# First and second down product of a block summed in PSUM, and the down products reordered

## The chip, the cores and the metric

The kernel runs on one core of one Trainium2 chip. The metric is the time of one execution in microseconds on the device, as the median of several runs. One execution was also taken by the hardware profiler; all views below are of that execution. The engines are named as in the profile: PE is TensorE's matmul, PEld its weight load, DVE is VectorE, ACT is ScalarE, POOL is GpSimd and SP is SyncE, which issues most loads.

## The reference

Input is x of 2048 rows and 512 columns. It is normalised by rows (layer norm without weights), and then two things are computed of it and joined. All is in 32-bit floats.

```python
xn = layernorm(x)
a  = einsum("sd,ed->se", xn, dft_hid_re)
b  = einsum("sd,ed->se", xn, dft_hid_im)
s  = dft_seq_re @ a - dft_seq_im @ b          # 2048 x 2048 matrices
g  = (sigmoid(xn @ w_gate) * (xn @ w_up)) @ w_down   # 512 -> 1792 -> 512
out = x + s * silu(g)
```

## The kernel before

**Exactness.** Every 32-bit operand of a matmul is split into a high and a low part: `split` (lines 73 and 74) rounds the value on ScalarE (`hi`) and takes the rest on VectorE (`lo`). A product is then three matmuls, hi by hi, hi by lo and lo by hi (`mm3`, lines 77 to 79). Each has 128 x 128 weights and 512 columns.

**Fewer products.** All large products are done as 2 x 2 blocks with seven block products instead of eight (the scheme of Strassen and Winograd). In the code, the seven are named 1, 6, 7, 4 (a chain that adds up in one place and is read after some of its steps), 2 (which goes on from product 1) and 5, 3 (a second chain). The sums and differences of the operands are made on VectorE (`combine`, line 129).

**Memory.** SBUF is a pool of 54 pages of 4 KB a partition (`page`); a page is used again when its last reader is done. PSUM has eight banks (`bank`): ga, ua, gb, ub, gc and uc for the chains a, b and c of the gate and up products, and two named pd for down products.

**Stages.** First 35 us normalise and turn half of the rows and do the first group of features. Then come 13 blocks (`BLOCKS`), each for one half h of the rows (1024) and one group g of 256 of the 1792 features. After them the DFT along the sequence (`seq_units`, four chunks), then that along the hidden dimension (`hidden_units`), which also multiplies with silu(g) and adds x.

**A block** (`block`) is seven units, one for each of the gate and up products in the order 1, 5, 2, 6, 7, 4, 3. A unit is twelve matmuls, six into a bank of g and six into one of u. After product 1, `seed` (line 475) copies ga and ua into gb and ub, so that product 2 can go on there. After products 6 and 7, `snap` (line 469) copies ga and ua into a page, and the next product goes on in ga and ua; `gate` (line 484) and `times` (line 487) form sigmoid(g) * u.

**Down products.** The gated block results of a block are multiplied with w_down while the next block runs: each unit of a block ends in one down product of the block before. For nearly all blocks this job is a `Seven`: seven products, each of six matmuls into the two pd banks. `SEVEN` gives their order. `run` does one; it takes new pd banks for products 2, 1 and 5 and goes on in the old ones for the others. After each product `gather` (line 309) copies both banks into a page on ScalarE, and POOL issues a DMA of 512 KB (line 311, or 314 the first time) that adds the page to one of eight parts of g in DRAM, g_part. Products 1 and 2 go to the same part (0, 0).

**Order.** The order of the instructions on every engine is written out by hand. `units` is a list of what TensorE does; `add` appends one with the operands it needs. Two units ahead of its use an operand is split, five ahead it is loaded. `sooner(n, f)` and `after(n, f)` put a step f before or after unit n. `Seven.spread` places the steps of a job relative to the first unit n of its own block: the differences and the splits of w_down (`Down.spread`; `raw` is the split of w_down itself, `dif` of its four differences), the four sums t1 to t4 of the gated results (`self.sums`), and the splits of the operands of products 6, 7 and 4. The list `waiting` holds the down products still to do; a job's seven are put there at unit 1 of the next block, and each unit takes the first one. What is left after the last block is done in chunk 0 of the DFT, after each second step of a product (`left` in `seq_units`).

**Other stores of POOL** that the prediction names: `i_part` (line 782) keeps operands of an inner product of the DFT, `s_part` (line 685) holds sums of xn, `f_part` (line 869) takes results of the first DFT, and `put_x` (line 1017) copies x into the output. SP's loads are of line 88.

Of the kernel before, what the change touches and what calls it, by code (L numbers as in the profile page):

```python
# [11 lines left out]
AF = mybir.ActivationFunctionType  # L12
# [23 lines left out]
def fnet_glu_kernel(ctx: ExitStack, tc: tile.TileContext, x, x_t, c_re, c_im, w_h, w_gu, w_down, out):  # L36
    nc = tc.nc
# [11 lines left out]
    def bank(tag):  # L49
        return banks.tile([P, 512], F32, name=tag, bufs=2 if tag == "pd" else 1)  # L50
# [25 lines left out]
    def mm3(ps, ws, ms, first, last, go_on=False):  # L76
        nc.tensor.matmul(ps, ws[0], ms[0], start=first, stop=False, skip_group_check=go_on)  # L77
        nc.tensor.matmul(ps, ws[0], ms[1], start=False, stop=False, skip_group_check=go_on)  # L78
        nc.tensor.matmul(ps, ws[1], ms[0], start=False, stop=last, skip_group_check=go_on)  # L79
# [235 lines left out]


    GATED = {(0, 0): 1, (0, 1): 2, (1, 0): 4, (1, 1): 3}
    SEVEN = (1, 6, 7, 4, 2, 5, 3)
    waiting = []

    class Plain:
# [23 lines left out]
        def run(self, n):  # L345
            b, i = divmod(n, 2)
            outs = []
            for o in range(2):
                at = slice((2 * i + o) * P, (2 * i + o + 1) * P)
                outs.append(bank("pd"))  # L350
                for f in range(2):
                    mm3(outs[-1], [t[:, at] for t in self.weights(f)], self.hs[f, b].get(), f == 0, f == 1)
            gather((2 * self.h + b) * 2 + i, outs)
# [13 lines left out]
    class Down:  # L367
# [21 lines left out]

        def spread(self, n, late):  # L390
            sooner(n + 4 * late - 4, self.wdl.load)
            for i, f in zip((4, 5, 6, 8) if late else (0, 2, 3, 5), (lambda: self.diffs(0), lambda: self.diffs(1), self.raw.get, self.dif.get)):
                after(n + i, f)

    class Seven:
# [2 lines left out]
        items, at = SEVEN, range(7)  # L398

        def __init__(self, h, wd, made):  # L400
            self.first, self.s, self.ps, self.made = 4 * h, {}, None, made
            self.raw, self.dif, self.wd = wd.raw, wd.dif, wd
            value = lambda k: lambda: self.s[k][:, 0, :]
            b11, b12, b21, b22 = (value(k) for k in (1, 2, 4, 3))

            def total(k, a, b):
                return Value([], lambda: combine(self.s[k][:, 1, :], a(), b(), ADD))

            t1 = total(1, b11, b12)
            t2 = total(3, t1.get, b22)  # L410
            t3 = total(2, b12, b22)
            t4 = total(4, t2.get, b21)
            self.sums = t1, t2, t3, t4
            src = {1: b11, 5: t1.get, 6: t2.get, 3: b22, 7: t3.get, 2: b21, 4: t4.get}
            self.h = {k: Parts([], v, [SB], joint=True) for k, v in src.items()}

        def spread(self, n, late):

            if not self.made:
                self.wd.spread(n, late)  # L420
            self.last = n == 7 * (len(BLOCKS) - 1)
            for i, v in zip((9, 11, 14, 17) if self.last else (7, 7, 8, 9), self.sums):
                sooner(n + i, v.get)
            if not self.last:
                for i, v in (8, self.dif), (8, self.h[6]), (9, self.h[7]), (10, self.h[4]):
                    sooner(n + i, v.get)

        def needs(self, k):

            if k in (6, 7, 4) and not self.last:  # L430
                return []
            return [self.h[k], self.dif if k in (5, 6, 7, 3) else self.raw]

        def weights(self, k):
# [2 lines left out]
            j, i = {1: (0, 0), 2: (1, 0), 4: (1, 1)}[k]  # L437
            return [t[:, j, i * D // 2 : (i + 1) * D // 2] for t in self.raw.get()]

        def run(self, k):  # L440
            first = k in (2, 1, 5)
            if first:
                self.ps = [bank("pd") for _ in range(2)]
            hv, wv = self.h[k].get(), self.weights(k)
            for o, ps in enumerate(self.ps):
                mm3(ps, [t[:, o * P : (o + 1) * P] for t in wv], hv, first, True, go_on=not first)
            (b, i), sign = {
                2: ((0, 0), 1),
                1: ((0, 0), 1),
                6: ((1, 0), -1),  # L450
                7: ((1, 1), -1),
                4: ((0, 1), 1),
                5: ((1, 1), 1),
                3: ((1, 0), 1),
            }[k]
            gather(self.first + 2 * b + i, self.ps, sign)

    def block(h, w, made, before, job, late):

        s, ps = job.s, {}  # L460
        n = len(units)
        if not made:
            for i, v in zip((-3, 0, 1, 3), w["s"]):
                sooner(n + i, v.get)

        def snap(k):
            s[k] = page([2, SB], F32)
            for m, c in enumerate("gu"):
                nc.scalar.activation(s[k][:, m, :], ps[c + "a"], AF.Copy)  # L469

        def seed():

            for c in "gu":
                ps[c + "b"] = bank(c + "b")
                nc.scalar.activation(ps[c + "b"], ps[c + "a"], AF.Copy)

        def plus(k):
            for m, c in enumerate("gu"):
                nc.vector.tensor_add(s[k][:, m, :], s[k][:, m, :], ps[c + "c"])

        def gate(k, tag=None):
            if tag:
                s[k] = page([2, SB], F32)
            nc.scalar.activation(s[k][:, 0, :], ps["g" + tag] if tag else s[k][:, 0, :], AF.Sigmoid)

        def times(k, tag=None):
            nc.vector.tensor_mul(s[k][:, 0, :], s[k][:, 0, :], ps["u" + tag] if tag else s[k][:, 1, :])

        tail = {1: seed, 6: lambda: snap(2), 7: lambda: (snap(3), plus(3)), 3: lambda: plus(2)}
        CH = {1: "a", 5: "c", 2: "b", 6: "a", 7: "a", 4: "a", 3: "c"}  # L490

        def unit(k, d):
            first = k in (1, 5)
            for m, c in enumerate("gu"):
                tag = c + CH[k]
                if first:
                    ps[tag] = bank(tag)
                product(k, ps[tag], w, h, m, first)
            if k in tail:
                tail[k]()  # L500
            if d:
                d[0].run(d[1])
            if k in (2, 4):
                gate({2: 1, 4: 4}[k], CH[k])
            if k in (7, 3):
                gate({7: 3, 3: 2}[k])
            if k == 4:
                times(4, "a")

        for i, k in enumerate((1, 5, 2, 6, 7, 4, 3)):  # L510
            if i == 1:
                waiting.extend((before, d) for d in before.items)
            d = waiting.pop(0) if waiting and i in waiting[0][0].at else None
            add([xop[h, k], w[k]] + (d[0].needs(d[1]) if d else []), lambda k=k, d=d: unit(k, d))
        sooner(n + 3, lambda: times(1, "b"))
        sooner(n + 5, lambda: times(3))
        sooner(n + 7, lambda: times(2))
        job.spread(n, late)
        return job
# [443 lines left out]

    def seq_units(job, c_sums):
        ops = a_operands()
        left = waiting + [(job, k) for k in SEVEN]
        n = len(units)
        after(n + 40, lambda: nc.scalar.activation(warm, mhalf, AF.Silu))
        for q in range(2):
            sooner(n - 9 + 4 * q, ops[1, q].load)  # L970
            sooner(n - 5 + 4 * q, ops[1, q].get)
        inner_a([n + i for i in (-43,-41,-38,-36,-34,-31,-27,-24,-20,-6,-3)])
        chunks = [Chunk(i, c_sums) for i in range(NT)]
        starts = []
        pair = None
        for tc_, plan in enumerate(PLAN):
            starts.append(len(units))
            c = chunks[tc_]
            done = dict.fromkeys(CHAIN, 0)
            for t in plan.replace(" ", ""):  # L980
                if t in "abcdefg":
                    if pair is None or pair.ended():
                        pair = Inner(*chunks[tc_ // 2 * 2 :][:2])
                    pair.step("abcdefg".index(t) + 1)
                    continue
                k = int(t)
                c.step(ops, k, done[k])
                done[k] += 1
                if left and done[k] % 2 == 0:
                    last_down(*left.pop(0))  # L990
        assert not left
        blocks = [Load(w_h[i, j], [4, D // 2]) for i in range(2) for j in range(2)]
        sums_ahead(diffs, blocks, w_part, range(starts[2] + 5, starts[2] + 9), 4)
# [148 lines left out]
    with tc.manual_schedule():  # L1142
        job, begin = start(0, 0)
# [102 lines left out]
```

## Time and profile before

| what | value |
|---|---|
| median of 3 runs | 804.81 us (804.71 to 805.5) |
| profiled execution | 804.79 us, span 803.0 us |
| PE busy | 794.5 us, 3594 matmuls |
| PEld busy | 658.1 us |
| DVE busy | 704.8 us |
| ACT busy | 535.9 us |
| POOL busy | 129.6 us |
| stores to g_part | 95, 512 KB each |
| granted TensorE clock | 1.00 in all windows |

The span goes from the first to the last instruction of the program; the time of the execution holds what lies around it too. Busy time is the time in which at least one instruction of an engine runs. In the list of groups, the columns are line, engine, operation, output and input, shape and count; then busy time and mean duration of one; then the idle time of the engine just before these instructions, with what ended it. The chain of waits follows the last instruction back to what released it, step by step.

### The profile page before, as it was taken

The numbers are of one execution on the slowest core, as the hardware profiler recorded it, in microseconds if no ns is written. First come the engines' busy times: TensorE is split into PE (matmuls) and PEld (weight loads), VectorE is DVE, ScalarE is ACT, GpSimd is POOL, SyncE is SP. The second block draws the span as 40 slices with busy tenths as digits, with TensorE's granted clock in tenths as the row PEclk, the third lists the DMA queues.
The fourth block names the chain that finished last, engine by engine and source line by source line (L and its number), as shares of the span: only waits on it lengthen the run. The fifth ranks groups of instructions, "written<-read, shape, count | busy, mean of one in ns | idle before, by whom it ended". The sixth has DMA issues, their size and how long they took to land.

```text
span 803.0 us, 10266 instructions
## 1 busy us (share of the span) xinstructions
PE 794.5 (99%) x3594; PEld 658.1 (82%) x3594; DVE 704.8 (88%) x917; ACT 535.9 (67%) x831; POOL 129.6 (16%) x179
## 2 busy tenths in 40 slices
PE   9999999999999999999999999999999999999997
PEld 8988888888888888788888887888887888888886
DVE  6878889889988998888989698999698899888986
ACT  4676888889777888777987855553545645548371
POOL 2002443222221223222211100001110000000201
PEclk9999999999999999999999999999999999999999
DMA  8153999997988999998999898429977585874826
GB/s 276 42 205 94 227 222 225 226 188 133 183 183 290 194 264 258 289 244 167 232 301 292 221 326 304 136 90 335 396 268 256 206 300 189 303 267 163 202 60 105
DMA packets 51139, 177.89 MB, mean 222 GB/s; under 512 B 5648, under 2 KB 5904, under 8 KB 51088
## 3 DMA queue, kind: packets, MB, share of 16 engines
q0 software_dynamic: 21696, 75.52, 43.6%
q1 hardware_dynamic: 29312, 101.66, 35.7%
q8 instruction: 28, 0.46, 0.2%
q14 instruction: 23, 0.19, 0.1%
q10 hardware_dynamic: 80, 0.07, 0.0%
HBM read 104.86 MB, written 76.03 MB: 225 GB/s over the span
## 4 chain that ended last, share of the span: by engine, by line
PE 94%; DMA 2%; DVE 2%; issue 1%; ACT 0%; DVEq 0%; ACTq 0%
PE pd L79 6%; PE pd L78 6%; PE pd L77 6%; PE ga L77 6%; PE ga L78 6%; PE ga L79 6%; PE ua L78 5%; PE ua L79 5%; PE ua L77 5%; PE gc L78 3%; PE gc L79 3%; PE uc L78 3%; PE uc L79 3%; PE uc L77 3%; PE gc L77 3%; PE gb L78 3%
## 5 line engine op out<-in xcount | busy, mean ns | idle before, releaser
L74 DVE TENSOR_TENSOR page<-page 128x512 fp32r<-128x512 f32 (+2 forms) x405 | 369.3, 943 | 49.7 <-ACT page L73 49.0
L73 ACT ACTIVATE page<-page 128x512 fp32r<-128x512 f32 (+2 forms) x405 | 316.4, 833 | 121.6 <-DVE page L129 112.6
L129 DVE TENSOR_TENSOR page<-page 128x512 f32<-128x512 f32 (+2 forms) x272 | 220.6, 827 | 1.3
L309 ACT ACTIVATE page<-pd 128x512 f32<-128x512 f32 x190 | 111.6, 599 | 57.5 <-PE pd L79 45.4
L311 POOL DMA_DIRECT2D g_part<-page x87 | 74.1, 852 | 274.5 <-ACT page L309 228.6
L79 PE MATMUL pd<-page 128*128 128x512 f32 x230 | 89.6, 390 | 0.0
L78 PE MATMUL pd<-page 128*128 128x512 f32 x230 | 89.5, 389 | 0.0
L77 PE MATMUL pd<-page 128*128 128x512 f32 x230 | 89.5, 389 | 0.0
L77 PE MATMUL ga<-page 128*128 128x512 f32 x200 | 78.2, 391 | 1.0 <-ACT page L469 1.0
L78 PE MATMUL ga<-page 128*128 128x512 f32 x200 | 78.0, 390 | 0.0
L79 PE MATMUL ga<-page 128*128 128x512 f32 x200 | 77.8, 389 | 0.0
L78 PE MATMUL ua<-page 128*128 128x512 f32 x196 | 76.4, 390 | 0.1
L77 PE MATMUL ua<-page 128*128 128x512 f32 x196 | 76.3, 389 | 0.0
L79 PE MATMUL ua<-page 128*128 128x512 f32 x196 | 76.3, 389 | 0.0
L79 PEld LDWEIGHTS pd<-page 128*128 128x128 f32 x230 | 43.2, 188 | 9.1 <-DVE page L74 0.3
L78 PEld LDWEIGHTS pd<-page 128*128 128x128 f32 x230 | 43.2, 188 | 9.0
L77 PEld LDWEIGHTS pd<-page 128*128 128x128 f32 x230 | 43.2, 188 | 9.0
L78 PE MATMUL gc<-page 128*128 128x512 f32 x124 | 48.6, 392 | 0.0
L78 PE MATMUL gb<-page 128*128 128x512 f32 (+1 forms) x126 | 48.4, 384 | 0.1
L79 PE MATMUL gc<-page 128*128 128x512 f32 x124 | 48.4, 390 | 0.1
L78 PE MATMUL uc<-page 128*128 128x512 f32 x124 | 48.3, 389 | 0.0
L79 PE MATMUL uc<-page 128*128 128x512 f32 x124 | 48.3, 389 | 0.0
(150 smaller groups left out, 1272.0 us busy)
## 6 DMA issues: line engine op xcount, KB each, us to landing
g_part<-page POOLq DMA_DIRECT2D x95, 512.0 KB, 6.8
page<-in_c_re_dram SPq DMA_DIRECT2D x49, 512.0 KB, 5.5
page<-in_c_im_dram SPq DMA_DIRECT2D x33, 512.0 KB, 7.1
page<-in_w_gu_dram SPq DMA_DIRECT2D x26, 512.0 KB, 6.8
f_part<-page POOLq DMA_DIRECT2D x16, 512.0 KB, 5.4
page<-f_part SPq DMA_DIRECT2D x16, 512.0 KB, 3.6
page<-i_part SPq DMA_DIRECT2D x14, 512.0 KB, 4.3
page<-in_w_down_dram SPq DMA_DIRECT2D x13, 512.0 KB, 6.0
```

The lines of the kernel that those rows point to most:

```text
L73: nc.scalar.activation(hi, src, AF.Copy)
L74: nc.vector.tensor_tensor(lo, src, hi.bitcast(F32), op=SUB)
L77: nc.tensor.matmul(ps, ws[0], ms[0], start=first, stop=False, skip_group_check=go_on)
L78: nc.tensor.matmul(ps, ws[0], ms[1], start=False, stop=False, skip_group_check=go_on)
L79: nc.tensor.matmul(ps, ws[1], ms[0], start=False, stop=last, skip_group_check=go_on)
L129: (engine or nc.vector).tensor_tensor(dst, a, b, op=op)
L309: nc.scalar.activation(pg[:, o, :], po, AF.Copy, scale=float(sign))
L311: nc.gpsimd.dma_start(g_part[i], pg, accum_op=ADD)
```

## The change

Product 1 of a Seven no longer goes to DRAM by itself. After it, a new `seed` copies the two pd banks into gb and ub, product 2 goes on adding there, and one `gather` from gb and ub stores the sum of both. So a Seven has six gathers instead of seven. For this the order changes to 5, 3, 1, 2, 6, 7, 4 (for the last block 1, 2, 6, 7, 4, 5, 3), and a job's products are put on the list `waiting` at unit 2 of the next block, where the job before is a Seven. Accordingly `dif` is split before `raw`, the sums and the splits ahead get other places (`S4`, `L4`, `H4`), product 5's operand is split ahead too, and the steps of chunk 0 and chunk 1 that are followed by a left-over down product are written out in `LEFT`, as the count of steps of the chunk.

```diff
-    SEVEN = (1, 6, 7, 4, 2, 5, 3)
+    SEVEN = (5, 3, 1, 2, 6, 7, 4)
+    LATE = 4, 5, 6, 8
+    LEFT = 2,4,6,8,10,12,14
+    L4 = 9, 11, 14, 17
+    S4 = 7,8,10,11
+    H4 = 8, 10, 11, 12
+    SEVEN_LAST = (1, 2, 6, 7, 4, 5, 3)
...
-            for i, f in zip((4, 5, 6, 8) if late else (0, 2, 3, 5), (lambda: self.diffs(0), lambda: self.diffs(1), self.raw.get, self.dif.get)):
+            for i, f in zip(LATE if late else (0, 2, 3, 5), (lambda: self.diffs(0), lambda: self.diffs(1), self.dif.get, self.raw.get)):
...
-            for i, v in zip((9, 11, 14, 17) if self.last else (7, 7, 8, 9), self.sums):
+            for i, v in zip(L4 if self.last else S4, self.sums):
                 sooner(n + i, v.get)
             if not self.last:
-                for i, v in (8, self.dif), (8, self.h[6]), (9, self.h[7]), (10, self.h[4]):
+                for i, v in zip(H4, (self.h[5], self.h[6], self.h[7], self.h[4])):
                     sooner(n + i, v.get)
...
+            if k == 5 and not self.last:
+                return [self.dif]
...
+        def seed(self):
+            self.ps["b"] = [bank(c + "b") for c in "gu"]
+            for ps, b in zip(self.ps["pd"], self.ps["b"]):
+                nc.scalar.activation(b, ps, AF.Copy)
+
         def run(self, k):
-            first = k in (2, 1, 5)
+            ch = "b" if k == 2 else "pd"
+            first = k in (1, 5)
             if first:
-                self.ps = [bank("pd") for _ in range(2)]
+                self.ps[ch] = [bank("pd") for _ in range(2)]
             hv, wv = self.h[k].get(), self.weights(k)
-            for o, ps in enumerate(self.ps):
+            for o, ps in enumerate(self.ps[ch]):
                 mm3(ps, [t[:, o * P : (o + 1) * P] for t in wv], hv, first, True, go_on=not first)
+            if k == 1:
+                self.seed()
+                return
...
-            gather(self.first + 2 * b + i, self.ps, sign)
+            gather(self.first + 2 * b + i, self.ps[ch], sign)
...
-            if i == 1:
+            if i == 1 + isinstance(before, Seven):
                 waiting.extend((before, d) for d in before.items)
...
-        left = waiting + [(job, k) for k in SEVEN]
+        left = waiting + [(job, k) for k in SEVEN_LAST]
...
-                if left and done[k] % 2 == 0:
+                if left and sum(done.values()) in LEFT:
                     last_down(*left.pop(0))
```

More of the change, by code (lines that the diff above doesn't have):

```diff
@@ L400, in __init__ @@
         def __init__(self, h, wd, made):
-            self.first, self.s, self.ps, self.made = 4 * h, {}, None, made
+            self.first, self.s, self.ps, self.made = 4 * h, {}, {}, made
             self.raw, self.dif, self.wd = wd.raw, wd.dif, wd
@@ L438, in weights @@
             return [t[:, j, i * D // 2 : (i + 1) * D // 2] for t in self.raw.get()]
+        def seed(self):
+            self.ps["b"] = [bank(c + "b") for c in "gu"]
+            for ps, b in zip(self.ps["pd"], self.ps["b"]):
+                nc.scalar.activation(b, ps, AF.Copy)
         def run(self, k):
-            first = k in (2, 1, 5)
+            ch = "b" if k == 2 else "pd"
+            first = k in (1, 5)
             if first:
-                self.ps = [bank("pd") for _ in range(2)]
+                self.ps[ch] = [bank("pd") for _ in range(2)]
             hv, wv = self.h[k].get(), self.weights(k)
-            for o, ps in enumerate(self.ps):
+            for o, ps in enumerate(self.ps[ch]):
                 mm3(ps, [t[:, o * P : (o + 1) * P] for t in wv], hv, first, True, go_on=not first)
+            if k == 1:
+                self.seed()
+                return
             (b, i), sign = {
                 2: ((0, 0), 1),
-                1: ((0, 0), 1),
                 6: ((1, 0), -1),
```

## The prediction

> **What bounds the kernel now.** I read the page's first two parts, then the windows, TensorE's list of waits, and the chain of waits where it leaves TensorE. First the page's span and busy times, then two 40 us windows (columns: window, length, busy us and instruction count of PE, PEld, DVE, ACT, POOL, granted clock, DMA share, GB/s), then TensorE's waits.
>
> ```profile
> span 803.0 us, 10266 instructions
> PE 794.5 (99%) x3594; PEld 658.1 (82%) x3594; DVE 704.8 (88%) x917; ACT 535.9 (67%) x831; POOL 129.6 (16%) x179
> ...
> 320.00:360.00 40.00, 39.03 (x173) 31.87 (x172) 35.45 (x56) 30.94 (x57) 8.20 (x10) 1.00 1.04 267
> 360.00:400.00 40.00, 40.00 (x178) 33.14 (x177) 35.05 (x58) 33.73 (x62) 9.04 (x11) 1.00 0.92 194
> ...
> PE gc L575 <- DVE ones L55: 1.4, 1, 1.4
> PE ga L77 <- ACT page L469: 1.0, 1, 1.0
> ```
>
> TensorE holds the time: at full clock it starts 178 matmuls in 40.00 us, one every 0.225 us, and a change that leaves its 3594 matmuls alone can win only what it waits. After the start it waits visibly once, 1.0 us, in 320 to 360 us, which has 173 matmuls instead of 178. The chain of waits tells why (columns: start, us, what):
>
> ```profile
> 324.99 0.24 PE pd L79
> 325.23 0.02 issue
> 325.25 0.61 ACT page L309
> 325.86 0.45 issue
> 326.31 11.38 DMA g_part<-page
> 337.69 0.02 issue
> 337.72 0.02 ACTq L469
> 337.73 0.04 issue
> 337.78 0.61 ACT page L469
> 338.38 0.04 issue
> 338.43 0.50 PE ga L77
> 338.93 0.23 PE ga L78
> ```
>
> A down product's result is copied out of PSUM (L309) and stored by an accumulating DMA (L311), which took 11.38 us to land. The 54 pages of SBUF are all in use, and ScalarE's next copy of ga (L469, the snapshot of the gate product) takes just that store's page. TensorE needs ga empty for the next product. The first matmul after the wait takes 0.50 instead of 0.23 us, so the wait costs 1.0 + 0.27, about 1.25 us. Other places are smaller; these are single matmuls of the chain that should take 0.23:
>
> ```profile
> 222.96 0.44 PE ga L77
> ...
> 451.88 0.46 PE gc L78
> ...
> 484.82 0.35 PE ga L78
> ...
> 490.19 0.50 PE ga L77
> ```
>
> They hold 0.21 + 0.23 + 0.12 + 0.27 = 0.83 us. All later stalls lie in stages whose instruction order the change leaves as it is.
>
> **The change part by part.** The sum is made against the profiled execution: 804.79 us, its span of 803.0 and 1.8 around it; the median of the runs is 804.81, so no correction is needed. The groups (columns: instruction, count, busy us, mean ns of one, idle before) and the DMA rows that price the parts:
>
> ```profile
> L309 ACT ACTIVATE page<-pd 128x512 f32<-128x512 f32 x190 | 111.6, 599 | 57.5 <-PE pd L79 45.4 <-issue 2.6 <-DMA g_part<-page 2.3
> L475 ACT ACTIVATE gb<-ga 128x512 f32<-128x512 f32 x13 | 7.5, 580 | 0.0
> L475 ACT ACTIVATE ub<-ua 128x512 f32<-128x512 f32 x13 | 7.2, 551 | 0.9 <-PE ua L79 0.9
> L469 ACT ACTIVATE page<-ga 128x512 f32<-128x512 f32 x26 | 15.4, 593 | 2.5 <-DMA g_part<-page 1.6 <-DMA i_part<-page 0.6 <-PE ga L79 0.2
> L311 POOL DMA_DIRECT2D g_part<-page x87 | 74.1, 852 | 274.5 <-ACT page L309 228.6 <-ACT page L73 24.2 <-ACT page L484 13.4
> q0 software_dynamic: 21696, 75.52, 43.6%
> q1 hardware_dynamic: 29312, 101.66, 35.7%
> g_part<-page POOLq DMA_DIRECT2D x95, 512.0 KB, 6.8
> page<-in_c_re_dram SPq DMA_DIRECT2D x49, 512.0 KB, 5.5
> page<-in_c_im_dram SPq DMA_DIRECT2D x33, 512.0 KB, 7.1
> DMA to landing us min/median/max: 2.9/6.7/12.1
> 300.00:338.00 38.00, 37.45 (x166) 30.69 (x164) 33.96 (x58) 29.93 (x57) 9.54 (x13) 1.00 1.05 274
> ```
>
> *TensorE.* Each Seven still has seven products of six matmuls; product 2 goes on adding in gb and ub instead of opening a pd pair. Count and sizes stay: 0 us.
>
> *ScalarE.* There are 13 Sevens. Each loses one pair of L309 copies (599 ns) and gains a pair of seeds, pd to gb and ub. No row shows a copy from pd into gb; the nearest, gb from ga and ub from ua, take 580 and 551. 26 x 599 = 15.6 against 26 x 566 = 14.7 us: 0.9 us less, on an engine that is 67% busy, off the path. Bounds: 551 to 599 ns a copy, so 0 to 1.2 us less. A seed stands where the copy stood, and its user, product 2, comes after twelve matmuls (2.7 us) of the next unit, against 1.1 to 1.2 us for two copies: hidden, and 1.5 us remain for splits queued ahead. Behind the seed in ScalarE's queue stand the gate and the next splits, as behind the copy before. gb and ub are free there: the block's own product in b is gated two units earlier, and the next block's seed comes three units later.
>
> *POOL and the DMA engines.* 13 accumulating stores of 512 KB vanish (95 to 82). POOL's 13 x 0.85 us are off the path. For the DMA engines: q0 is busy 0.436 x 803 = 350 us for 144 transfers of 512 KB, q1 0.357 x 803 = 287 us for 194, so 1.5 us each. Of q0's, 94 accumulate (87 of L311, 7 of the output); if the other 50 cost what q1's do, an accumulation costs (350 - 75)/94 = 2.9 us of all 16 engines, an estimate. A block of seven units of 18 matmuls lasts 28.4 us, and its stores take 20 us of that; one less takes a tenth of the blocks' DMA load away. It matters where the DMA share is 1.05, from 300 to 338 us, and there the stall lies.
>
> *The stall at 337 us.* In the built programs the snapshot at this place takes another page: before, one released by a gather's store 46 matmuls earlier; after, one released by a VectorE split 25 matmuls (5.6 us) earlier, with no DMA in it. So this wait goes whatever the DMA does: -1.25. What is late next is the snapshot one unit on, whose page comes from an i_part store in both programs. It was at its limit before; POOL's issue of that store and the copy that waited for it, in the timelines:
>
> ```profile
> 332.67 0.56 POOL L782 DMA_DIRECT2D i_part<-page  x1 [0.26 <-DVE page L74]
> ...
> 341.91 0.60 ACT L469 ACTIVATE page<-ga 128x512 f32<-128x512 f32 x1 [0.64 <-DMA i_part<-page]
> ```
>
> The store landed 9.2 us after its issue, and the copy came at once. Afterwards 35 matmuls (7.9 us) lie between, not 37, and TensorE no longer loses 1.25 us ahead of it. The six down matmuls (1.35 us) less the copy (0.59) give a slack of 0.75, so with the same landing the wait is 9.2 + 0.4 - 7.9 - 0.75, about 1.0 us. But since 300 us one or two accumulations fewer, 3 to 6 us of DMA work, stand ahead of it. I take 0, and keep 1.0 as the bound.
>
> *Order of the sums and splits.* The down products start one unit later, and t2, t3 and t4 spread over five units instead of three. In the built programs the nearest split of a down product's operands stands 18 matmuls ahead of its use inside the blocks, 14 before. Two places come nearer by two matmuls, 0.45 us: a weight split of product 2 of the gate and up products (13 ahead, 2.9 us) and the L309 copies before the next use of pd (8, 1.8 us, where ScalarE needs 1.2). Both keep 0.6 us or more to spare, so 0 in the blocks; if that cover goes, each block loses at most these 0.45 us.
>
> *The end of the blocks.* Two products (7 and 4) are left over instead of one, and chunk 0 takes seven downs, so products 5 and 3 of the last Seven move into chunk 1, some 210 matmuls (47 us) later. Their operands and the split weights hold four pages for that time. SP's loads then find their page later: the stretch from a free page to first use shrinks from about 58 to 45 matmuls, 10 us against the median landings of the loads there, 5.5 and 7.1 us: still covered. Two store pages are reused 27 matmuls (6.1 us) after the store, 32 and more before; by the median landing of 6.8 plus 0.4 us for the issue ScalarE or VectorE waits up to 1.1 us there, ahead of the split at 451.88, which has no slack. One split before 482 us comes two matmuls (0.45 us) nearer to its user. Bounds 0 to +1.5; I take +0.2, near the low end, since 32 matmuls (7.2 us) before left only 0.4 us over that landing and the place cost 0.23 us. put_x and f_part stores queue behind two later gathers on POOL (1.7 us); their readers come over 100 us later: 0.
>
> Sum: 804.8 - 1.25 + 0.2 = 803.7.
>
> **The rivals.** *Further relief.* The lighter DMA also clears the small stalls up to 490 us: 804.8 - 1.25 - 0.83 = 802.7. For it: all DMA work until 470 us shrinks, and the places at 222.96 and 490.19 are first products on ga, where TensorE waits for a snapshot as at 337. Against it: in the built programs the splits at 451.88 and 484.82 stand as near to their users as before.
>
> *The pages run out elsewhere (slower).* Between 325 and 345 us three store pages are reused after 39, 35 and 35 matmuls (8.8, 7.9 and 7.9 us), where one landing took 11.38 us. If the smaller load does not shorten that, the i_part snapshot waits 11.4 + 0.4 - 7.9 - 0.75 = 3.2 us of TensorE: 803.7 + 3.2 = 806.9. It decides from a landing of about 10.9 us on. For it: a store of i_part landed only after 9.2 us, the share is 1.05, and SP's w_gu load now waits for such a landing. Against it: less traffic, and landings fall after 338. The Trainium skill's page "Perfetto Trace Analysis", section "Optimization Strategy", says that a gap that comes again and again on the engine that should be full can mean too little SBUF for the next tile; by this rule longer-held pages would multiply the stall and this rival would win. The trace shows only one such gap, so it gets no more than the chance below.
>
> *Hidden anyway.* The 1.25 us return at the i_part snapshot (1.0) and the end of the blocks: 804.8.
>
> **How the numbers follow.** 0.2%, 1.6 us, is about what a measurement of this kernel can tell from no change, so faster means below 803.2 and slower above 806.4. Chances: forecast 0.38, further relief 0.34, pages elsewhere 0.22, hidden anyway 0.06. Same is 0.38 + 0.06 = 0.44. The likeliest case's own range is 803.2 to 805.0. The full range goes from 802.5, just under the relief, to 807.0, just over the page rival, and leaves out some 0.1 at each end or less.
>
> **What would show it.** After: g_part x82; L309 on 164 copies; 26 new copies into gb and ub at 0.55 to 0.60; 178 matmuls in 320 to 360 us; no wait of TensorE for the snapshot; fewer MB on q0 (68.7). A snapshot that waits for i_part, or new gaps on TensorE between 440 and 500 us, would show which rival came. The forecast is wrong if TensorE's waits before 440 us sum to over 1 us, or if the time falls below 803.2 because small stalls went.

## The result and the profile after

The changed kernel takes 806.37 us in the median (805.33 to 810.37), the kernel before 805.11 us (804.12 to 806.75) beside it, 22 runs each. The ratio is 1.0018 with a 95% interval of 1.0012 to 1.0024: slower by 1.3 us, where 1.1 us faster was forecast. The range of 802.5 to 807.0 held it.

What the change should do to the instructions it did. First lines of the page of the changed kernel, its group of copies, its DMA row, and the new copies (`seed`, line 451 in the new file; copies and stores keep lines 309 and 311, the snapshot has line 485) from the answer on that line:

```profile
span 804.3 us, 10251 instructions
PE 795.8 (99%) x3594; PEld 657.8 (82%) x3594; DVE 703.1 (87%) x917; ACT 535.7 (67%) x831; POOL 121.1 (15%) x166
...
q0 software_dynamic: 19824, 68.70, 39.5%
...
L309 ACT ACTIVATE page<-pd 128x512 f32<-128x512 f32 x138 | 81.3, 599 | 50.4 <-PE pd L79 44.8
...
g_part<-page POOLq DMA_DIRECT2D x82, 512.0 KB, 6.4
...
L451 ACT ACTIVATE gb<-pd x13: 582/582/652, 82.8 to 426.2; 128x512 f32<-128x512 f32 x13
L451 ACT ACTIVATE ub<-pd x13: 573/582/617, 83.4 to 426.9; 128x512 f32<-128x512 f32 x13
```

There are 82 stores, 138 copies out of pd and 26 more out of gb and ub, and 26 seeds of 0.58 us. Yet TensorE, which holds the time, needs 1.25 us longer until its last matmul ends (797.44 before, 798.69 after). Two windows of the kernel before, and four of the kernel after (window, length, busy us and count of PE, PEld, DVE, ACT, POOL, clock, DMA share, GB/s), show where:

```profile
40.00:80.00 40.00, 40.00 (x179) 33.10 (x178) 32.58 (x49) 27.48 (x48) 6.06 (x10) 1.00 0.47 149
...
480.00:520.00 40.00, 39.99 (x176) 32.27 (x175) 36.11 (x34) 21.86 (x24) 1.26 (x2) 1.00 0.65 237
```

```profile
40.00:80.00 40.00, 39.94 (x176) 32.76 (x175) 30.93 (x47) 27.51 (x48) 5.69 (x8) 1.00 0.41 142
320.00:360.00 40.00, 40.00 (x178) 32.88 (x177) 33.67 (x53) 32.49 (x59) 8.23 (x10) 1.00 0.97 235
360.00:400.00 40.00, 39.78 (x176) 32.56 (x175) 36.16 (x60) 33.04 (x62) 7.34 (x9) 1.00 0.87 186
480.00:520.00 40.00, 39.25 (x168) 30.77 (x167) 33.04 (x32) 22.96 (x28) 2.88 (x4) 1.00 0.78 243
```

The wait at 337 us is gone: 178 matmuls in 320 to 360 us instead of 173. Three other windows lost matmuls, the one from 480 to 520 us eight of them.

Part of the difference lies outside the span. The time of an execution is the span and what lies around it: 2.09 to 2.20 us in all 22 runs of the changed kernel, and 1.72 to 1.85 us in the runs of the kernel before beside the experiments. So some 0.35 of the 1.26 us are no wait of TensorE; no run shows what makes them.

For all kernels below I added up the lost time of TensorE in the profiled execution, from 30 us on: over all matmuls, by how much the next one started later than 0.227 us after it (the usual distance), where that was over 0.06 us. In us, by stretch:

| kernel | 30-320 | 320-380 | 380-440 | 440-495 | 495-550 | 550-end | sum |
|---|---|---|---|---|---|---|---|
| before | 0.21 | 1.24 | 0 | 0.61 | 0 | 1.74 | 3.81 |
| after | 0.33 | 0.60 | 0 | 0.61 | 1.64 | 1.72 | 4.91 |

So 1.45 us were won (337 and 222 us) and 2.57 us lost: 0.33 at 70 us, 0.11 at 340 us, 0.49 at 368 us and 1.64 from 505 to 516 us. The chain of waits of the changed kernel shows all but the 0.11 (start, us, what):

```profile
70.52 0.70 DVE page L74
...
71.26 0.50 PE gb L79
...
357.83 8.79 DMA g_part<-page
...
366.70 0.07 ACT page L309
...
368.72 0.61 ACT page L485
...
369.37 0.50 PE ga L77
...
496.69 7.66 DMA g_part<-page
...
504.45 0.07 ACT page L73
...
507.27 7.68 DMA g_part<-page
...
515.04 1.24 DVE page L74
...
516.32 0.50 PE gc L78
```

At 70 us (0.33) a split on VectorE ends too late for gb: `dif`, which the change splits first, puts a 1024-wide split ahead of it. At 340 us (0.11) it is the snapshot that the prediction kept at its limit: ScalarE waits 1.63 us for the store to i_part, and TensorE loses little by it. At 368 us (0.49) the copies of a gather take the page of a store issued 31 matmuls before, which needed 8.79 us to land, and the snapshot queued behind them is late. From 505 to 516 us (1.64) it is the stores of products 5 and 3 of the last Seven, now in chunk 1: two splits of the DFT take their pages 32 and 34 matmuls after, and the stores landed after 7.66 and 7.68 us.

### The profile page after: what moved, and what is told of

Read it like the earlier page. It is cut to its first block, busy times and chain, and to the rows that moved or that the text cites. A ratio compares the mean times of both kernels' runs of the same rounds, so it can differ in the third digit from the quotient of the medians.

```text
span 804.3 us, 10251 instructions
## 1 busy us (share of the span) xinstructions
PE 795.8 (99%) x3594; PEld 657.8 (82%) x3594; DVE 703.1 (87%) x917; ACT 535.7 (67%) x831; POOL 121.1 (15%) x166
## 4 chain that ended last, share of the span: by engine, by line
PE 89%; issue 3%; DMA 3%; DVE 2%; ACT 1%; POOL 0%; ACTq 0%; DVEq 0%; POOLq 0%
PE pd L79 5%; PE pd L78 5%; PE pd L77 5%; PE ga L77 5%; PE ga L78 5%; PE ga L79 5%; PE ua L78 5%; PE ua L79 5%; PE ua L77 5%; PE gb L79 4%; PE gb L78 4%; PE gb L77 4%; PE gc L78 3%; PE gc L79 3%; PE uc L78 3%
## 5 line engine op out<-in xcount | busy, mean ns | idle before, releaser
L74 DVE TENSOR_TENSOR page<-page 128x1024 fp32r<-128x1024 f32 (+2 forms) x405 | 371.4, 943 | 70.9 <-ACT page L73 70.1
L73 ACT ACTIVATE page<-page 128x1024 fp32r<-128x1024 f32 (+2 forms) x405 | 316.9, 833 | 127.0 <-DVE page L129 112.7
L129 DVE TENSOR_TENSOR page<-page 128x512 f32<-128x512 f32 (+2 forms) x272 | 220.0, 827 | 1.2 <-DMA page<-in_w_gu_dram 0.4
L309 ACT ACTIVATE page<-pd 128x512 f32<-128x512 f32 x138 | 81.3, 599 | 50.4 <-PE pd L79 44.8
L311 POOL DMA_DIRECT2D g_part<-page x74 | 63.3, 855 | 273.6 <-ACT page L309 251.1
L79 PE MATMUL pd<-page 128*128 128x512 f32 x204 | 79.5, 390 | 0.0
L77 PE MATMUL pd<-page 128*128 128x512 f32 x204 | 79.4, 389 | 0.0
L78 PE MATMUL pd<-page 128*128 128x512 f32 x204 | 79.4, 389 | 0.0
L78 PE MATMUL gb<-page 128*128 128x512 f32 (+1 forms) x139 | 53.5, 385 | 0.1
L79 PE MATMUL gb<-page 128*128 128x512 f32 (+1 forms) x139 | 53.4, 384 | 0.1
L77 PE MATMUL gb<-page 128*128 128x512 f32 (+1 forms) x139 | 53.2, 383 | 0.0
L78 PE MATMUL ub<-page 128*128 128x512 f32 x131 | 51.1, 390 | 0.0
L77 PE MATMUL ub<-page 128*128 128x512 f32 x131 | 51.0, 389 | 0.0
L79 PE MATMUL ub<-page 128*128 128x512 f32 x131 | 51.0, 389 | 0.0
```

The costliest lines, as they stand in the source:

```text
L73: nc.scalar.activation(hi, src, AF.Copy)
L74: nc.vector.tensor_tensor(lo, src, hi.bitcast(F32), op=SUB)
L129: (engine or nc.vector).tensor_tensor(dst, a, b, op=op)
L309: nc.scalar.activation(pg[:, o, :], po, AF.Copy, scale=float(sign))
L311: nc.gpsimd.dma_start(g_part[i], pg, accum_op=ADD)
```

## The experiments

Edits are against the changed kernel unless another is named. The ratio is to the kernel before, on the same chip.

**First group: which part costs what.** No store in chunk 1, with all nine left-over products in chunk 0:

```diff
-    LEFT = 2,4,6,8,10,12,14
+    LEFT = 1,2,4,6,8,10,12,14,16
```

> The changed kernel, but all nine left-over down products are done in chunk 0 (after steps 1, 2, 4, 6, ... 16 of it) instead of seven there and two in chunk 1. Theory (the two late stores: their pages are taken again after 32 and 34 matmuls, before the stores land, and TensorE stops for the split that waits): the 1.6 us of stalls between 504 and 517 us go, and the time falls from 806.4 to about 804.8, level with before. Rival (the seeds and the new order cost the time inside the blocks): stays at 806.0 or more.

Measured: 806.77 us, ratio 1.0021 (1.0013 to 1.0030). A miss: nothing was stored in chunk 1, and it still lost 1.34 us there. ScalarE's timeline of this kernel, and then of the kernel before, tells why:

```profile
499.67 1.28 ACT L984 ACT_TABLE_LOAD   x1
500.96 0.20 ACT L984 ACTIVATE warm<-mhalf 128x1 f32<-128x1 f32 x1
501.07 1.99 ACT L73 ACTIVATE page<-page 128x1024 fp32r<-128x1024 f32 x2
```

```profile
499.22 1.05 ACT L73 ACTIVATE page<-page 128x1024 fp32r<-128x1024 f32 x1
500.29 1.28 ACT L968 ACT_TABLE_LOAD   x1
```

`after(n + 40)` counts units, and a left-over product is one. With nine of them ahead of it, one more than in the other two kernels, the 1.28 us load of a table for ScalarE's next function (`ACT_TABLE_LOAD`) came out ahead of a split instead of behind it. So the experiment changed two things.

Only the two late stores taken away, with their copies kept:

```diff
+            gather(..., sign, not (self.last and k in (5, 3)))
```

> The changed kernel, but the two stores of the last two down products (5 and 3 of the last job, in chunk 1) are left out; their matmuls, splits and copies stay where they are. Theory (the landing of these stores): stalls between 504 and 517 us go, about 804.8. Rival (the extra splits and copies of these two products keep VectorE and ScalarE too busy in chunk 1, and the pages they hold delay loads): the stalls stay, 806.0 or more.

Measured: 804.69 us, ratio 0.9998 (0.9989 to 1.0007), against 1.0018 with them. Its window has the count of the kernel before again:

```profile
480.00:520.00 40.00, 39.99 (x176) 32.54 (x175) 35.07 (x34) 23.91 (x29) 1.25 (x2) 1.00 0.64 227
```

So these two stores alone make the change slower rather than even. Two rows of the changed kernel, ScalarE's and VectorE's, show the splits that took their pages (in brackets the idle time before and what ended it):

```profile
504.45 1.06 ACT L73 ACTIVATE page<-page 128x1024 fp32r<-128x1024 f32 x1 [2.85 <-DMA g_part<-page]
...
515.04 1.23 DVE L74 TENSOR_TENSOR page<-page 128x1024 fp32r<-128x1024 f32 x1 [0.26 <-DMA g_part<-page]
```

The second wait is short because VectorE comes to it late already. Its split that starts at 498.12 us without the two stores starts at 497.20 with them; after the first wait the same pair of times is 505.74 and 506.69, and at the split above 513.92 and 515.04. So VectorE fell 1.87 us behind by the first wait, did not make it up, and stood 2.04 us behind after the second. By this, most of the 1.64 us is the first store's.

Up to 490 us this program is the same as the changed one, and yet it lost 1.42 us in 320 to 380 and 1.22 in 440 to 495, where the other trace has 0.60 and 0.61. How late a store lands differs from one execution to the next: the one issued near 358 us landed after 8.79 us in the changed kernel's trace and after 9.38 in this one, the one near 441 us after 6.19 and 6.94. So single stalls under some 0.8 us in those stretches are not to be compared between two traces.

The new order without the sum in PSUM, each product with a store of its own:

```diff
-    SEVEN = (5, 3, 1, 2, 6, 7, 4)
+    SEVEN = (5, 3, 2, 1, 6, 7, 4)
...
-            ch = "b" if k == 2 else "pd"
-            first = k in (1, 5)
+            ch = "pd"
+            first = k in (1, 2, 5)
...
```

> The new order and the delay of one unit alone: products 1 and 2 each have their own pd banks and their own store again (order 5, 3, 2, 1, 6, 7, 4), so there are 95 stores and no seeds. Theory (the sum in PSUM helps by lightening the DMA engines, the loss is the order's): chunk 1's stalls stay, and store pages in the blocks are taken again after 29 to 36 matmuls under the old DMA load: 807.0 to 808.5, landings at 320 us of 10 us and more. Rival (the sum in PSUM is what costs): 805.5 or less.

Measured: 817.07 us, ratio 1.0146 (1.0131 to 1.0162). The direction is right, the size is not: 10.7 us over the change. Its windows, and a step of its chain:

```profile
125.00:134.00 9.00, 9.00 (x41) 7.44 (x41) 3.45 (x6) 2.50 (x6) 4.50 (x5) 1.00 1.06 224
134.00:141.00 7.00, 2.31 (x10) 1.28 (x8) 5.38 (x6) 5.90 (x11) 0.84 (x1) 0.88 0.81 140
141.00:146.00 5.00, 5.00 (x12) 3.95 (x13) 5.00 (x9) 2.89 (x6) 0.84 (x1) 0.50 1.00 211
...
126.83 9.21 DMA g_part<-page
```

With 95 stores this order loses 11.8 us before 380 us, 2.4 of them at a halved clock (last section); with 82 it loses 0.9. In this order the pages are wanted too soon for seven stores a block, and the store that the change saves pays for the order. The kernel before, with its own order, carried seven a block at 1.45 us.

Products again from unit 1 of the next block, so that none is left for chunk 1:

```diff
-    LEFT = 2,4,6,8,10,12,14
+    LEFT = 2,4,6,8,10,12,14,16
-    S4 = 7,8,10,11
-    H4 = 8, 10, 11, 12
+    S4 = 7,7,9,10
+    H4 = 8, 9, 10, 11
-            if i == 1 + isinstance(before, Seven):
+            if i == 1:
```

> The sum in PSUM and the new order, but without the delay: a job's products begin at unit 1 of the next block as before, with the sums and splits ahead moved up by one unit, so one product is left over and all eight are done in chunk 0. Theory (the loss hangs on the two products that the delay pushes into chunk 1): no stall between 500 and 520 us and no new one in the blocks, 803.6 to 804.5. Rival (product 5 needs the sum t1, which is ready too late for unit 1): each of 12 blocks loses 0.3 us or more, 808 and above.

Measured: 807.8 us, ratio 1.0037 (1.0025 to 1.0050), the rival's side. Two windows, of this kernel and of the changed one, and the chain of this kernel:

```profile
90.00:150.00 60.00, 59.89 (x263) 48.95 (x263) 53.54 (x89) 49.64 (x88) 20.35 (x25) 1.00 0.90 201
...
97.93 1.82 DVE page L74 x3
...
99.79 0.50 PE pd L78
```

```profile
90.00:150.00 60.00, 60.00 (x266) 49.71 (x265) 53.53 (x89) 50.59 (x90) 19.68 (x25) 1.00 0.94 211
```

Product 5 now comes first and waits for the split of its operand, 0.32 to 0.42 us in each of six blocks (2.72 us are lost until 320 us, 0.40 of it at 70 us). The one unit of delay is what makes the order cheap there, and it is what leaves two products over. What this version loses from 380 to 495 us, 2.45 us more than the changed kernel, was not followed.

**Second group: the table load and the splits.** All in chunk 0, with the table load behind the split again:

```diff
-    LEFT = 2,4,6,8,10,12,14
+    LEFT = 1,2,4,6,8,10,12,14,16
-        after(n + 40, ...
+        after(n + 41, ...
```

> All nine left-over products in chunk 0, and ScalarE's table load for silu one unit later. It is placed by a count of units; the ninth left-over product moved it one unit nearer to the start, from behind a split of 128x1024 to ahead of it, where it held that split back by 1.5 us. Theory (this made the stalls at 503 to 517 us of the run with all nine in chunk 0): they go, 1.3 us less, 805.4. Rival (nine products in chunk 0 are too much for VectorE and ScalarE): stays at 806.5 or more.

Measured: 804.49 us, ratio 1.0000 (0.9992 to 1.0009). Nothing is lost in 495 to 550 us, so the table load was the 1.34. But 0.53 us come at 410 us, where a left-over product after step 1 stands ahead of the gate's split:

```profile
408.99 1.24 DVE page L74
...
410.27 0.50 PE ga L78
```

The same, with the splits ahead one unit later and the last block's `raw` split before `dif`:

```diff
-    H4 = 8, 10, 11, 12
+    H4 = 8, 11, 12, 13
```

> As the run before it in this list, and the operand splits of products 6, 7 and 4 one unit later (places 8, 11, 12, 13), so that each holds its page a unit less, and in the last block raw split before dif as in the kernel before. In the program no store's page is then taken again in the blocks before 35 matmuls; 31 to 36 at eight places without it. Theory (pages taken again before their store lands cause the stalls at 340 and 368 us): these go (1.0 us) with that at 410 us (0.5 us), and the kernel ends below before: 803.5 to 804.3. Rival (the splits come too late for TensorE now): 805.5 or more.

Measured: 805.23 us, ratio 1.0003 (0.9995 to 1.0012). A miss: the losses in 320 to 380 us went (0), those at 410 us did not (0.72), nor those in 440 to 495 (1.27). Its median lies 0.74 us above that of the version before, though its trace lost less; 0.32 us of it lie outside the span (2.10 beside 1.78 us).

The cross test: the kernel before with nothing but its table load one unit earlier.

```diff
-        after(n + 40, ...
+        after(n + 39, ...
```

> The kernel before the change, with nothing but the table load for silu one unit earlier, so that it stands ahead of the same split. Theory (the table load's place costs what the run with all nine in chunk 0 lost there): 805.1 + 1.3 = 806.4, with stalls between 503 and 517 us. Rival (it is hidden): 805.1.

Measured: 806.79 us, ratio 1.0020 (1.0011 to 1.0029), as expected. Its window:

```profile
480.00:520.00 40.00, 39.46 (x169) 30.94 (x168) 34.68 (x33) 20.80 (x23) 1.27 (x2) 1.00 0.67 243
```

It loses 1.35 us in 495 to 550 us, where the kernel before loses nothing. Moving one 1.28 us instruction past one split costs as much as the change as a whole.

The late splits alone on the changed kernel:

```diff
-    H4 = 8, 10, 11, 12
+    H4 = 8, 11, 12, 13
```

> The changed kernel with nothing but the operand splits of products 6, 7 and 4 one unit later. Theory: the stalls near 340 and 368 us go, 0.6 us, those in chunk 1 (1.6 us) stay: 805.8. Rival (the stall at 368 us has another cause than the page): 806.4.

Measured: 805.74 us, ratio 1.0012 (1.0003 to 1.0021), as expected: 0 lost in 320 to 380 us, and the loss in 495 to 550 stays (1.83).

**Third group: other places for the left-over products.** Late splits and late table load, all nine products in chunk 0 but none after step 1:

```diff
-    LEFT = 2,4,6,8,10,12,14
+    LEFT = 2,4,6,8,10,12,14,16,18
```

> The change, with three places altered: all nine left-over down products in chunk 0, after steps 2, 4, ... 18 (none after step 1); the load of the sigmoid's table for chunk 1 one unit later, so that it stays behind the 128x1024 split at 499 us; and the splits ahead (H4) at 8, 11, 12, 13. TensorE lost 3.81 us in stalls in the kernel before and 4.91 us after the change. Theory (each loss after the change is a page of a store that is wanted again some 31 to 34 matmuls later, or a split that comes too near its use): the stalls at 368 us (0.49) and between 505 and 515 us (1.64) go, the one at 409 us that came with a product after step 1 doesn't appear, and the one at 70 us (0.33) stays. Left: 4.91 - 0.49 - 1.64 = 2.8 us, that is 1.0 us less than before, some 804.0 us beside 805.0 of the kernel before, ratio 0.9987. Rival (in chunk 0 the products stand in front of splits wherever they are put, so the loss of 0.5 to 0.7 us near 410 and 0.3 us near 482 us comes back): 3.8 us of stalls, 805.0 us, ratio 1.000.

Measured: 804.68 us, ratio 0.9994 (0.9985 to 1.0003). The losses at 368, 410 and 505 to 516 us are gone. 1.07 us came at 480 us, where a 1024-wide split on VectorE is late; the sum is 3.81, that of the kernel before. The rival named that place, at 0.3 us, and its sum of 3.8; the time of 804.0 that the theory gave was missed, though the two lie too near to each other for the interval to tell.

The same with `dif` split one unit earlier in the blocks:

```diff
-    LATE = 4, 5, 6, 8
+    LATE = 4, 5, 5, 8
```

> As the version with the products after steps 2, 4, ... 18, and the split of the four differences of w_down in the first blocks one unit earlier (LATE 4, 5, 5, 8 in place of 4, 5, 6, 8). Theory (the 0.33 us stall at 70 us is the 1024-wide split of a difference that stands on VectorE ahead of the gate's split): that stall goes, 0.33 us less than that version, 803.7 us if that one takes 804.0, ratio to before 0.998. Rival (the 1024-wide split only stands ahead of another split there, with as little room): a stall of about the same size at another place between 60 and 75 us, and the same time.

Measured: 806.04 us, ratio 1.0020 (1.0011 to 1.0029), a miss for both. Its windows:

```profile
40.00:80.00 40.00, 40.00 (x178) 33.14 (x177) 33.33 (x52) 27.50 (x48) 6.73 (x10) 1.00 0.46 153
200.00:240.00 40.00, 39.37 (x173) 32.03 (x172) 36.01 (x52) 32.18 (x55) 7.90 (x10) 1.00 0.78 156
320.00:360.00 40.00, 39.51 (x175) 32.39 (x174) 34.56 (x55) 32.05 (x60) 8.19 (x10) 1.00 0.97 230
```

The 0.33 us at 70 us went as the theory said, so its cause is shown. But snapshots at 221, 337 and 366 us were late again, 0.90, 0.77 and 1.0 us. At 337 us the split ahead of the snapshot in ScalarE's queue had waited 0.69 us for a store's page; at 221 us its chain goes back through splits alone. That a split which comes a unit earlier also takes its pages a unit earlier would explain the first; no run shows it.

The two late products in chunk 1, with the late splits, in place of steps 2 and 4 first after steps 14 and 16:

```diff
-    LEFT = 2,4,6,8,10,12,14
+    LEFT = (2, 4, 6, 8, 10, 12, 14), (14, 16)
-                if left and sum(done.values()) in LEFT:
+                if left and sum(done.values()) in LEFT[tc_]:
```

> The change with the late splits (H4 at 8, 11, 12, 13), and the two down products left for chunk 1 after its steps 14 and 16 instead of 2 and 4. There the page of neither store is wanted again within 37 matmuls (8.5 us); after steps 2 and 4 they were wanted after 32 and 34. Theory (those two reuses are the 1.73 us of stalls between 505 and 515 us, since such a store lands 7.7 us after its issue): these stalls go and nothing comes for them, 805.7 - 1.7 = 804.0 us, ratio to before 0.999. Rival (stores among the first DFT products of chunk 1 cost TensorE as much wherever they stand, by the splits and snapshots that they delay): 1 to 2 us of stalls at a later place, 805 to 806 us, ratio 1.000 to 1.001.

Measured: 810.27 us, ratio 1.0065 (1.0052 to 1.0079). 6.01 us are lost in 495 to 550 us, none of it to a store. ScalarE's and then VectorE's timeline of this kernel (in brackets the idle time before and what ended it), beside a row of ScalarE's from the changed kernel:

```profile
509.58 1.06 ACT L73 ACTIVATE page<-page 128x1024 fp32r<-128x1024 f32 x1 [2.74 <-PE uc L78]
...
514.60 1.06 ACT L73 ACTIVATE page<-page 128x1024 fp32r<-128x1024 f32 x1 [2.38 <-PE uc L78]
...
529.70 1.23 DVE L74 TENSOR_TENSOR page<-page 128x1024 fp32r<-128x1024 f32 x1 [2.72 <-PE ua L78]
```

```profile
512.62 1.06 ACT L73 ACTIVATE page<-page 128x1024 fp32r<-128x1024 f32 x1 [2.08 <-DVE page L129]
```

The splits no longer wait for their input (L129) but for a matmul to give a page back: the products that stand over keep the pages of their operands and weights, and the rest of the pool does not reach.

Then after steps 8 and 10:

> The same with the two products after steps 8 and 10 of chunk 1. Their pages are wanted again after 23 matmuls each, 5.2 us. Theory: with a landing of 7.7 us the stall of each grows by the nine to eleven matmuls (2.0 to 2.5 us) by which the reuse comes earlier, unless the landing is quicker there; some 1.7 + 4.5 = 6.2 us of stalls in chunk 1, 808.5 us, ratio to before 1.005; with a landing of 5.5 us as for a lone store still 2 us, 806 us. Rival (the distance of the reuse doesn't decide): about what the other version with late stores loses, 804 to 805.7 us.

Measured: 804.55 us, ratio 0.9996 (0.9987 to 1.0005), where the theory said 806 to 808.5. The pages are wanted after 23 matmuls, sooner than in the changed kernel, and cost less. The DMA issues of the changed kernel from 490 to 520 us (count, KB each, median us to landing), then of this kernel the stores from 515 to 540 us, SyncE's loads in that time (start, us from the first issue to the last, count), and one row of ScalarE:

```profile
page<-in_c_im_dram SPq DMA_DIRECT2D x8, 512.0 KB, 5.0
g_part<-page POOLq DMA_DIRECT2D x2, 512.0 KB, 7.7
```

```profile
g_part<-page POOLq DMA_DIRECT2D x2, 512.0 KB, 5.5
...
523.46 12.69 SPq L811 DMA_DIRECT2D page<-i_part  x2
538.84 1.39 SPq L88 DMA_DIRECT2D page<-in_c_re_dram  x2
```

```profile
528.54 2.01 ACT L73 ACTIVATE page<-page 128x1024 fp32r<-128x1024 f32 x2 [1.33 <-DMA g_part<-page]
```

The two stores are issued at 522.7 and 527.5 us and have landed by 532.7. One load is under way beside them, the first of i_part; in the changed kernel there were eight in all. They land in 5.5 us instead of 7.7. The split that takes the first page does wait, 1.33 us, but no matmul is late for it. So how many matmuls lie between store and reuse does not decide alone; the landing at that place and the room behind the waiting split do. That the loads make the difference in landing is likely, but no run changed them alone. What this version loses in 495 to 550 us (1.22) comes before and beside these waits: 0.87 of it, at 526 us, is behind a split that waited 1.12 us for a matmul to give a page back, as in the version with steps 14 and 16.

Lost time of TensorE in these kernels, as in the table above:

| kernel | 30-320 | 320-380 | 380-440 | 440-495 | 495-550 | 550-end | sum | ratio |
|---|---|---|---|---|---|---|---|---|
| all in chunk 0 | 0.33 | 1.00 | 0.54 | 0.60 | 1.34 | 1.73 | 5.55 | 1.0021 |
| no late stores | 0.33 | 1.42 | 0 | 1.22 | 0 | 1.74 | 4.71 | 0.9998 |
| order alone | 8.56 | 3.28 | 0.11 | 0.33 | 1.97 | 1.72 | 15.97 | 1.0146 |
| no delay | 2.72 | 0.70 | 0.80 | 2.26 | 0.11 | 1.74 | 8.33 | 1.0037 |
| table later | 0.33 | 0.38 | 0.53 | 1.31 | 0 | 1.69 | 4.24 | 1.0000 |
| and late splits | 0.33 | 0 | 0.72 | 1.27 | 0 | 1.72 | 4.04 | 1.0003 |
| before, table earlier | 0.21 | 1.57 | 0 | 0.60 | 1.35 | 1.70 | 5.43 | 1.0020 |
| late splits alone | 0.33 | 0 | 0 | 0.60 | 1.83 | 1.73 | 4.50 | 1.0012 |
| even steps | 0.33 | 0 | 0 | 1.79 | 0 | 1.70 | 3.81 | 0.9994 |
| `dif` earlier | 1.41 | 1.77 | 0 | 1.79 | 0 | 1.73 | 6.69 | 1.0020 |
| steps 14, 16 | 0.33 | 0 | 0 | 0.62 | 6.01 | 1.72 | 8.68 | 1.0065 |
| steps 8, 10 | 0.33 | 0 | 0 | 1.14 | 1.22 | 1.72 | 4.41 | 0.9996 |

No version is measurably faster than the kernel before. Five (no late stores, table later, and late splits, even steps, steps 8 and 10) take back what the change lost: their intervals include 1.

## Why the prediction failed, step by step

*TensorE, ScalarE, POOL.* Right: 3594 matmuls, 26 seeds at 0.58 us (0.55 to 0.60 forecast), off the path. A store less costs the DMA engines less by (0.436 x 803.0 - 0.395 x 804.3)/13 = 2.5 us, 2.9 estimated.

*The stall at 337 us, -1.25.* Right: 178 matmuls in that window. The snapshot behind it, taken at 0 with a bound of 1.0, cost 0.11 us. The 0.21 us at 222 us went too, which only the relief rival had.

*Order of the sums and splits, 0 in the blocks.* Too low by 0.8 us. The step asked how far a split stands ahead of its use and whether the copies before the next use of pd have room. It did not ask, for the copies of each gather, whose page they take (0.49 us at 368 us, a store 31 matmuls before), nor what the wider split of `dif` does to the gate's split behind it (0.33 us at 70 us). The late splits show that the first goes when the page order shifts: the same store's page is then taken after 35 matmuls, and five traces with late splits lose nothing there (the sixth, with `dif` earlier, does), where the four traces with the places of the changed kernel lose 0.27 to 1.08 us.

*The end of the blocks, +0.2 with bounds 0 and +1.5.* This is the term that failed: 1.64 us. The step looked at the pages reused 27 matmuls after a store, ahead of 452 us. In the trace of the changed kernel those cost 0.22 us, as the place did before; in the trace without the late stores, where that store took 6.94 instead of 6.19 us to land, they cost 0.84. Pages wanted after 32 matmuls the step passed over, since 7.2 us covered the median landing of 6.8. The two stores of chunk 1 landed after 7.66 and 7.68 us, among eight loads, and behind the first wait stood both halves of a 1024-wide split (1.06 and 1.23 us) with 13 matmuls to the first user. That VectorE would carry that delay on to the splits behind it was not in the step. Without the two stores the time is that of the kernel before.

*The sum.* 1.44 us too little here and 0.93 in the blocks (0.33, 0.11 and 0.49), less 0.21 at 222 us: 803.7 + 2.16 = 805.86. The 1.8 us around the span, which the sum took over unchanged, are 2.13 in the median of the 22 runs; with these 0.33 us it is 806.2, against 806.37 in the median. The rest isn't resolved.

*The rivals.* "The pages run out elsewhere" had the mechanism, a store's page wanted before it lands, but named the stores between 325 and 345 us and 3.2 us at once. There the traffic did fall (DMA share 0.97 after 1.04) and only 0.11 us was lost at 340. That the range held the time is in part luck, since its upper end was that rival's price at a place where it was not paid. "Hidden anyway" had the end of the blocks as a place that takes back what is won, but reckoned no more than 804.8; of "further relief" only the 0.21 us came, the stalls at 451.88, 484.82 and 490.19 us stayed. The rule of the Trainium skill's page "Perfetto Trace Analysis", section "Optimization Strategy", that a repeated gap can mean too little SBUF, got too little weight. The traces agree with it: the changed kernel lost time at four matmuls within 10 us of chunk 1, and with the products kept until steps 14 and 16 at seven within 32 us, with splits that waited for pages.

## What to carry to other kernels

Where a pool of buffers is full and the order is written by hand, price every buffer that a store holds: the time to its next taker against the landing in that stretch (not the median of the kernel), plus the work that stands between the taker and the engine that sets the time. Work that is pushed out of a stage keeps its operands' buffers and brings its transfers to another stage's traffic; here what was won (1.45 us) was paid for at the place where the left-over went (1.64 us). An instruction that is placed by a count of units moves when a unit is added, so list what passes what on each engine before putting a change's cost down to the change.

## What the runs showed of the hardware

TensorE's list of waits of the version with the new order alone has one of 3.3 us, at 134 us:

```profile
PE pd L77 <- ACT page L309: 3.3, 1, 3.3
```

A second idle time of 1.4 us followed before 141 us. TensorE then ran its next 12 matmuls at one every 0.43 us, with a granted clock of 0.50 in the window from 141 to 146 us: 2.4 us lost beyond the idle time. The granted clock was 1.00 from 134 to 138 us and 0.73 from 138 to 141 us, so the step came after the long wait had ended. Of the four runs of that version this one, of 816.87 us, had a mean granted clock of 0.994; the fastest, of 815.26 us, had 0.999, and the runs of the other kernels have 0.998 to 1.000. A wait of 1.7 us at 344 us of this trace left the clock at 1.00, and so did those of up to 1.0 us after the start in the other kernels. The Trainium skill's page "TensorE: Matmul & The Clock Gate", section "What's actually happening", has such a step to half the clock after an idle window of about 3.4 us. This trace agrees in the size of the step, and its 3.3 us of idle time are near that figure; it does not show over which stretch the idle time counts.
